# Six units of attention and three pieces of the layers per section instead of four and two, with the rows of 1/rms issued from ScalarE's queue

## The chip, the cores and the metric

The kernel runs on one core of one Trainium2 chip. A core has five engines that each work through a queue of their own: TensorE (PE, with PEld for its weight loads), VectorE (DVE), ScalarE (ACT), GpSimd (POOL) and SyncE (SP), which issues transfers. The metric is the device time of one execution in microseconds (us). The kernel before takes 531.6 us, the median of three runs (530.16 to 532.11). Its profile is of one execution with a span of 526.9 us. All arithmetic is in 32-bit floats.

## The reference, cut to what matters

Two blocks follow each other. Eight batches, twelve heads, 448 tokens, heads of 64.

```python
def rmsnorm(x, g):
    rms = np.sqrt(np.mean(x * x, axis=-1, keepdims=True) + 1e-06)
    return x / rms * g
q_n, k_n = rmsnorm(q, g_q), rmsnorm(k, g_k)
scores = scale * q_n @ k_n^T ; attn = softmax(scores)
x = attn @ v                     # as (batch, 448 tokens, 768)

scores = np.einsum('bsd,d->bs', x, w_gate)
for b in range(B):               # mixture of depths: 128 tokens of each batch
    top_idx = np.argpartition(-scores[b], 128)[:128]
    xe = x[b, top_idx]
    ye = np.maximum(xe @ w1, 0.0) @ w2        # 768 -> 1024 -> 768
    out[b, top_idx] = xe + sigmoid(scores[b, top_idx])[:, None] * ye
```

Tokens that are not chosen keep `x`. The two layers `w1` and `w2` are applied to the 128 chosen tokens alone.

## The kernel before, in words

**Tiling.** The work of attention is cut into 24 groups (eight batches of three), each with four heads, and each group into seven units of 64 keys. A unit `u` has a part `scores(u)`: four matmuls of 64x64 tiles into two PSUM buffers of the pool `ps_sc` (four in all), and two exponentials on ScalarE (L298) that write `p` (seven buffers). A part `values(u)` multiplies `p` with the values into `ps_av`, and `add_probs(u)` adds `p` into the group's sums on VectorE (L335) or, early, on GpSimd. A float matmul shows as two rows in the trace, so two units make 16 rows of scores and 16 of values.

**After a group.** `values_out` copies the result from PSUM on ScalarE, `sum_keys` sums the denominators on TensorE (den_ps, L367), `invert_sums` transposes them and takes the reciprocal (denT_ps, L392 and L394), and `to_tokens` transposes the result into tokens (x_ps, L410) and scales it into `x` on VectorE (L412). `last_tokens` does this for the second half of the group and then plans `gate` (L436, four VectorE products), and for a batch's last group `store_x` (L424) and `spread`.

**After a batch.** `ranks_of` transposes the gate scores to rows (row_ps, L465), which ScalarE copies (score_rows, L469); `count` finds each token's rank on VectorE (L479); `select` scatters the best 128 tokens to DRAM from GpSimd; `load_selected` reads them back as `xe`. `mixture` applies the layers to them, and is a generator: it is cut into ten pieces by its `yield`s. Two pieces transpose `xe` (L547, copied to `xeT` by ScalarE, L552), four multiply with `w1` (L575, relu on ScalarE after every second, L584), four with `w2` (L595, the result into `xe` by VectorE after every second, L604). All of them but the second write into the single PSUM buffer `moe_ps`. The tiles x_ps (its first half), den_ps and row_ps likewise share the single buffer of `ps_aux`.

**Norms.** The keys' 1/rms is a scale of the exponential. The queries' 1/rms has to be spread over the partitions: `squares` (ScalarE, L207), `sum_squares` (VectorE sum, L214, and a power on GpSimd, L217, 2.69 us each), then `rows_out` writes the 7 KB of 1/rms to DRAM (L228), `rows_in` reads them back as `bc`, every row to 64 partitions (L239), and `scale_q` multiplies the queries with them on VectorE (L248). A wait stands between: the read is issued only when the write has landed. The first two groups do without DRAM, by small matmuls (`scale_q_early`).

**The order.** Nothing is reordered: each engine takes its instructions as the Python code emits them. The main loop goes by sections. A section `q` first emits scores and values of its units, two by two, values lagging by two units, and then as many pieces of a mixture as the section has halves. With `HALVES = 2` a section has `PER = 4` units and two pieces, and 168 units make 42 sections. Around the pieces stand `opening(q, place)`, which takes the next of the tasks after a group, and `run(slots)`, which emits what was planned with `at(slot, ...)`: a slot is a unit, and the slots of a half are emitted around that half's piece. `prepare` plans squares, sums, `rows_out` and `rows_in` of group `n` from a slot about 20 units ahead of its first score, and `scale_q` 6 units ahead of it (in the first groups, 11 slots after the squares). `piece` starts a mixture when its batch is ready; while `q in begin`, in the first sections, no mixture that is past its second piece goes on in a section's second half. Loads of tokens, queries, keys, values and weights, the store of `x`, and the rows of 1/rms all go through SyncE's queue.

Of the kernel before, what the change touches and what calls it, by code (L numbers as in the profile page):

```python
# [68 lines left out]
def fast(  # L69
# [21 lines left out]
    nc = tc.nc  # L91

    B, NP, _, S = loads.src["qT"].shape
    CP = 112
    NJ = S // CP
    D = 64
# [59 lines left out]
    for c in range(2):  # L156
        nc.vector.memset(pick_pair[D * c : D * (c + 1), c : c + 1], 1.0)
    nc.vector.scalar_tensor_tensor(
        out=gg, in0=loads.gcol[:, 0:1], scalar=scale, in1=loads.gcol[:, 1:2], op0=OP.mult, op1=OP.mult
# [43 lines left out]
    def squares(n, i):  # L203
        t = get("tok", n, i)
        sq = sqs[(2 * n + i) % 2]
        for h in [slice(0, 1), slice(1, 2)] if (n, i) == (0, 0) else [slice(0, 2)]:
            nc.scalar.activation(out=sq[:, h, :, 0:D], in_=t[:, h], func=AF.Square, scale=scale)  # L207
        sss[n, i] = norm_pool.tile([128, 2, NI], F32, name="ss", bufs=4)
        return sq

    def sum_squares(n, i, sq):
        ss = sss.pop((n, i))
        for h in [slice(0, 1), slice(1, 2)] if (n, i) == (0, 0) else [slice(0, 2)]:
            nc.vector.tensor_reduce(out=ss[:, h], in_=sq[:, h], axis=AX.X, op=OP.add)  # L214
        rinv = norm_pool.tile([128, 2, NI], F32, name="rinv", bufs=8)
        flat = "p h i -> p (h i)"
        nc.gpsimd.tensor_tensor(  # L217
            out=rinv.rearrange(flat),
            in0=ss.rearrange(flat),
            in1=neg_half.to_broadcast([128, 2 * NI]),  # L220
            op=OP.pow,
        )
        rinvs[n, i] = rinv

    def rows_out(n):

        rows = dram_pool.tile([2, 2 * S], F32, name="rows", bufs=3)
        nc.sync.dma_start(  # L228
            out=rows.rearrange("h (p i) -> p h i", i=NI), in_=rinvs.pop((n, 0))
        )  # L230
        bcs[n] = rows

    def rows_in(n):

        rows = bcs[n]
        bc = norm_pool.tile([128, 2, S], F32, name="bc")
        for hh in range(2):
            src = rows[hh].rearrange("(c s) -> c s", c=2)
            nc.sync.dma_start(  # L239
                out=bc[D * hh : D * (hh + 1)],  # L240
                in_=dataclasses.replace(src, ap=[[0, D]] + [list(x) for x in src.ap]),
            )
        bcs[n] = bc

    def scale_q(n):
# [153 lines left out]
    def to_tokens(n, c):  # L399
        b = n // NG  # L400
        if b not in xs:
            xs[b] = x_pool.tile([CP, NJ, DX], F32, name="x")
        t = xTs.pop((n, c))
        shape = [128, NJ, 128]
        if c == 1 and not before_layers(now[0]):
            ps = ps_sc.tile(shape, F32, tag="sc", name="x_ps")
        else:
            ps = aux(shape, "x_ps")
        for j in range(NJ):
            nc.tensor.transpose(out=ps[:CP, j, :], in_=t[:, j, :], identity=ident)  # L410
        col = (n % NG * 2 + c) * 128
        nc.vector.tensor_tensor(  # L412
            out=xs[b][:, :, col : col + 128].rearrange("p j (h d) -> p j h d", d=D),
            in0=ps[:CP].rearrange("p j (h d) -> p j h d", d=D),
            in1=rdens[n][:, :, :, c, None].to_broadcast([CP, NJ, 2, D]),
            op=OP.mult,
        )
# [208 lines left out]

    HALVES = 2
    PER = 2 * HALVES  # L630
    units = n_groups * NI
    todo, tasks = {}, []

    def at(slot, fn, *args):
        todo.setdefault(slot, []).append(lambda: fn(*args))
# [6 lines left out]
    def opening(q, place):  # L642
        now[:] = q, place
        for _ in range(2):
            for i, (when, fn) in enumerate(tasks[:2]):
                if when <= (q, place):
                    tasks.pop(i)
                    waited = len(dens)
                    fn()
                    if place == 0 and len(dens) < waited:  # L650

                        break
                    return
                if i == 0 and dens:

                    return

    def prepare(n, slot):
        sq = {}
        for i in range(2):  # L660
            at(slot + 2 * i, lambda i=i: sq.setdefault(i, squares(n, i)))
            at(slot + 2 * i + 1, lambda i=i: sum_squares(n, i, sq.pop(i)))

        at(slot + (7 if n > 2 else 6), rows_out, n)
        at(slot + (10 if n > 5 else 9 if n > 2 else 8), rows_in, n)

    for n in range(1, n_groups):
        s0 = NI * n
        if n > 2:
            at(max(s0 - 26, 4 * (n - 3)), load, "tok", n, 0)  # L670
            at(max(s0 - 26, 4 * (n - 3)), load, "tok", n, 1)
        if n > 1:
            at(max(s0 - 13, 2), load, "qT", n)
            at(max(s0 - 11, 2), load, "kT", n)
            at(max(s0 - 11, 2), load, "v", n)
            first = max(s0 - (20 if n > 5 else 17), 0)
            prepare(n, first)
            at(max(s0 - 6, first + 11), scale_q, n)
# [5 lines left out]
    def finish(n, q):  # L684

        if n == n_groups - 1:
            for fn, args in ((sum_keys, (n,)), (invert_sums, (n,)), (to_tokens, (n, 0))):
                task((q, 1), fn, *args)
            task((q, 1), last_tokens, n)
            return  # L690
        task((q, 1), sum_keys, n)
        task((q + 1, 0), to_tokens, n, 0)
        task((q + 1, 1), last_tokens, n)
# [10 lines left out]
    def soon():  # L704

        q, place = now
        return PER * q + 2 * place if PER * q < units else -9

    def last_tokens(n):
        to_tokens(n, 1)  # L710
        b, g = divmod(n, NG)
        s = soon()
        at(s, gate, n)
        if g < NG - 1:
            return
        at(s, store_x, b)
        at(s + 1, spread, b)
        q, place = now

        when = (q + 1 + place // 2, 0) if b < B - 1 else (q + 1, 1)  # L720
        tasks.insert(0, (when, lambda: ranks_of(b)))

    def ranks_of(b):
        score_rows(b)
        s = soon()
        at(s, count, b, (0, 1))
        at(s + 1, count, b, (2, 3))
        at(s + 2, annotate, b)
        at(s + 2, select, b)
        at(s + 8 if s >= 0 else s + 3, load_selected, b)  # L730
        ready[b] = max((s + 8) // PER + 1, first_ff(b) - 1 if b else 0) if b < B - 1 else 0

    def first_ff(b):


        return -(-(units + 2 * PER - NG * NI * (B - 2 - b)) // PER)
# [34 lines left out]
    def piece(q):  # L771

        nonlocal moe, done
        if q in begin and pieces[0] > 2 and half == 1:
            return False
        pieces[0] += 1
        if next(moe, moe) is not moe:
            return True
        if ready.get(done, q + 1) > q:
            return False  # L780
        moe = mixture(done)
        done += 1
        pieces[0] = 1
        next(moe)
        return True


    begin = range(first_ff(0) + 1)
    pieces = [0]
    waiting = list(range(units))  # L790
    moe, ready, done, q = iter(()), {}, 0, 0
    while done < B or tasks:
        now[:] = q, 0
        k = PER * q
        for half in range(HALVES):
            for u in (k + 2 * half, k + 2 * half + 1):
                if u < units:
                    scores(u)
            run_values(k + 2 * half - 1, q)
        opening(q, 0)  # L800
        for half in range(HALVES):
            slots = (k + 2 * half, k + 2 * half + 1)
            if not short(q):
                run(slots)
            some = piece(q)
            spare[0] = not some and half == 0
            if some or half == 0 or len(tasks) > 2:
                opening(q, half + 1)
            spare[0] = False
            run(slots)  # L810
        q += 1
# [533 lines left out]
```

## Time and profile before

| what | value |
|---|---|
| time, median of 3 | 531.6 us |
| span of the profile | 526.9 us |
| TensorE busy | 507.6 us, 96% |
| VectorE, ScalarE, GpSimd busy | 63%, 53%, 36% |
| attention on TensorE (L289, L313) | 154.8 and 147.1 us busy |
| layers on TensorE (`w1` L575 while attention runs, `w2` L595) | 69.3 and 61.3 us busy |
| share of the 16 DMA engines, 11 to 97 us | 0.84 |
| the same, 97 to 467 us | 0.55 |
| write of the rows, issue to landing | 5.4 us, median of 22 |
| read of the rows, issue to landing | 6.4 us, median of 44 |

The lengths of TensorE's rows overlap, because matmuls are pipelined; what a run of them costs is read from its start to the start of the next. In a row of the timeline stand its start, its length, the engine, the line, the operation, the tile it writes and those it reads, the shape, how many instructions are merged, and in brackets the idle time of the engine before it and what ended that. SPq rows are SyncE's issuing of transfers, not the transfers. The first 97 us have attention and loads alone, from 104 us on layers and attention alternate, and after 467 us the layers of the last two batches are left.

### The profile page before, as it was taken

The numbers are of one execution on the slowest core, as the hardware profiler recorded it, in microseconds if no ns is written. First come the engines' busy times: TensorE is split into PE (matmuls) and PEld (weight loads), VectorE is DVE, ScalarE is ACT, GpSimd is POOL, SyncE is SP. The second block draws the span as 40 slices with busy tenths as digits, with TensorE's granted clock in tenths as the row PEclk, the third lists the DMA queues.
The fourth block names the chain that finished last, engine by engine and source line by source line (L and its number), as shares of the span: only waits on it lengthen the run. The fifth ranks groups of instructions, "written<-read, shape, count | busy, mean of one in ns | idle before, by whom it ended". The sixth has DMA issues, their size and how long they took to land.

```text
span 526.9 us, 11121 instructions
## 1 busy us (share of the span) xinstructions
PE 507.6 (96%) x4482; PEld 298.8 (57%) x4482; DVE 334.2 (63%) x638; ACT 278.1 (53%) x507; POOL 191.8 (36%) x109
## 2 busy tenths in 40 slices
PE   6999997999999999999999999998999999999995
PEld 5544343565744476546654467644664448659694
DVE  4566879579846896658666787467947487336101
ACT  4886873857644845456644585645463474401100
POOL 4956866623512454132712424304621003002102
PEclk9999998999999999999999999999999999999998
DMA  8968779799764297526846396537542231104100
GB/s 304 382 217 291 244 224 345 251 291 340 200 187 161 82 291 232 163 94 192 260 136 183 87 297 211 159 103 223 195 131 71 70 136 31 31 1 143 53 32 35
DMA packets 43405, 93.21 MB, mean 177 GB/s; under 512 B 11059, under 2 KB 23348, under 8 KB 43346
## 3 DMA queue, kind: packets, MB, share of 16 engines
q1 hardware_dynamic: 39938, 86.11, 52.1%
q0 software_dynamic: 3264, 6.31, 3.5%
q8 instruction: 37, 0.61, 0.5%
q14 instruction: 22, 0.18, 0.1%
q10 hardware_dynamic: 144, 0.00, 0.0%
HBM read 74.93 MB, written 25.35 MB: 190 GB/s over the span
## 4 chain that ended last, share of the span: by engine, by line
PE 89%; DVE 4%; DMA 2%; ACT 2%; issue 2%; POOL 0%; DVEq 0%; SPq 0%; ACTq 0%; POOLq 0%
PE sc L289 24%; PE av L313 22%; PE moe_ps L575 13%; PE moe_ps L595 11%; PE sc L595 4%; PE x_ps L410 4%; PE sc L575 4%; PE den_ps L367 3%; DMA bc<-rows 2%; PE denT_ps L392 1%; ACT p L298 1%; DVE sum L335 1%; PE warm_ps L164 1%; DVE ss L214 1%; DVE x L412 1%
## 5 line engine op out<-in xcount | busy, mean ns | idle before, releaser
L298 ACT ACTIVATE p<-sc,rinv 128x448 f32<-128x448 f32 x336 | 186.6, 642 | 106.3 <-PE sc L289 92.5
L217 POOL TENSOR_TENSOR rinv<-ss,neg_half 128x14 f32<-128x14 f32 x48 | 128.8, 2689 | 198.3 <-DVE ss L214 170.6
L289 PE MATMUL sc<-qT,kT 64*64 64x448 f32 x1344 | 154.8, 549 | 1.1 <-DVE qT L268 0.4
L313 PE MATMUL av<-p,v 64*64 64x448 f32 x1344 | 147.1, 537 | 0.0
L335 DVE TENSOR_TENSOR sum<-sum,p 128x896 f32<-128x896 f32 x101 | 111.6, 1105 | 7.2 <-ACT p L298 0.9
L313 PEld LDWEIGHTS av<-p,v 64*64 64x64 f32 x1344 | 60.1, 133 | 67.6 <-issue 56.9
L289 PEld LDWEIGHTS sc<-qT,kT 64*64 64x64 f32 x1344 | 54.3, 133 | 70.9 <-issue 47.0
L214 DVE TENSOR_REDUCE ss<-sq 128x14 f32<-128x910 f32 (+1 forms) x49 | 52.4, 1074 | 33.9 <-ACT sq L207 33.9
L575 PE MATMUL moe_ps<-xeT,w 128*128 128x128 f32 x576 | 69.3, 277 | 0.0
L575 PEld LDWEIGHTS moe_ps<-xeT,w 128*128 128x128 f32 x576 | 66.2, 192 | 5.3 <-issue 5.3
L595 PE MATMUL moe_ps<-w,hT 128*128 128x384 f32 x176 | 61.3, 491 | 0.4 <-DVE xe L604 0.3
L412 DVE TENSOR_TENSOR x<-x_ps,rden 112x512 f32<-112x512 f32 x48 | 32.8, 690 | 37.2 <-PE x_ps L410 36.4
L506 POOL DMA_INDIRECT selected<-x,rank x32 | 33.6, 1050 | 47.3 <-DVE x L498 39.3
L207 ACT ACTIVATE sq<-tok 128x896 f32<-128x896 f32 (+1 forms) x49 | 46.4, 951 | 5.7 <-DMA tok<-in_tok_dram 3.7
L595 PEld LDWEIGHTS moe_ps<-w,hT 128*128 128x128 f32 x176 | 31.7, 190 | 22.5 <-issue 2.5
L436 DVE SCALAR_TENSOR_TENSOR prod<-x,wg 112x256 f32<-112x256 f32 x96 | 41.5, 432 | 3.0
L614 POOL DMA_INDIRECT out_dram<-xe,row x10 | 11.6, 1164 | 81.1 <-DVE rden L394 47.3
L410 PE MATMUL x_ps<-ident,xT 128*112 128x128 f32 x192 | 29.5, 279 | 3.3 <-DVE rden L394 3.3
L335 DVE TENSOR_TENSOR sum<-p 128x896 f32<-128x896 f32 x24 | 25.9, 1078 | 5.2 <-ACT p L298 5.2
L604 DVE SCALAR_TENSOR_TENSOR xe<-sc,xe 128x384 f32<-128x384 f32 (+1 forms) x6 | 3.3, 550 | 40.6 <-PE sc L595 40.6
L410 PEld LDWEIGHTS x_ps<-ident,xT 128*112 128x112 f32 x192 | 21.8, 135 | 12.6 <-issue 7.7
L248 DVE SCALAR_TENSOR_TENSOR qT<-qT,gg,bc 128x896 f32<-128x896 f32 x22 | 25.2, 1147 | 5.1 <-DMA bc<-rows 5.1
(71 smaller groups left out, 311.0 us busy)
## 6 DMA issues: line engine op xcount, KB each, us to landing
tok<-in_tok_dram SPq DMA_DIRECT2D x48, 448.0 KB, 6.3
qT<-in_qT_dram SPq DMA_DIRECT2D x24, 448.0 KB, 6.2
kT<-in_kT_dram SPq DMA_DIRECT2D x24, 448.0 KB, 7.0
v<-in_vp_dram SPq DMA_DIRECT2D x24, 448.0 KB, 7.7
out_dram<-x SPq DMA_DIRECT2D x8, 1344.0 KB, 7.8
bc<-rows SPq DMA_DIRECT2D x44, 224.0 KB, 6.4
xe<-selected SPq DMA_DIRECT2D x8, 385.0 KB, 3.1
w<-in_moe_w_dram SPq DMA_DIRECT2D x6, 512.0 KB, 6.4
```

Of the source, the lines that this page charges most:

```text
L207: nc.scalar.activation(out=sq[:, h, :, 0:D], in_=t[:, h], func=AF.Square, scale=scale)
L214: nc.vector.tensor_reduce(out=ss[:, h], in_=sq[:, h], axis=AX.X, op=OP.add)
L217: nc.gpsimd.tensor_tensor(out=rinv.rearrange(flat), in0=ss.rearrange(flat), in1=neg_half.to_broadcast([128, 2 * NI]), op=OP.pow,)
L289: nc.tensor.matmul(out=scs[hh][D * c : D * (c + 1), 0:S], lhsT=get("kT", n)[r, c, D * i : D * (i + 1)], rhs=get("qT", n)[r, c, :], start=True,
L298: nc.scalar.activation(out=p[:, hh], in_=scs[hh][:, 0:S], func=AF.Exp, scale=rinvs[n, 1][:, hh, i : i + 1],)
L313: nc.tensor.matmul(out=avs[n][c][D * hh : D * (hh + 1), 0:S], lhsT=get("v", n)[r, hh, i, :], rhs=probs[u][r, hh], start=(i == 0), stop=(i ...
L335: nc.vector.tensor_tensor(out=sums[n], in0=probs.pop(u - 1) if begins else sums[n], in1=probs.pop(u), op=OP.add)
L410: nc.tensor.transpose(out=ps[:CP, j, :], in_=t[:, j, :], identity=ident)
L412: nc.vector.tensor_tensor(out=xs[b][:, :, col : col + 128].rearrange("p j (h d) -> p j h d", d=D), in0=ps[:CP].rearrange("p j (h d) -> p j ...
L436: nc.vector.scalar_tensor_tensor(out=prod, in0=xs[b][:, j, cols], scalar=1.0, in1=wg[:, cols], op0=OP.mult, op1=OP.mult, accum_out=gates[b ...
L575: nc.tensor.matmul(out=ps[:, 128 * i : 128 * i + n], lhsT=w1[:, dc, 128 * (f0 + i) : 128 * (f0 + i + 1)], rhs=xeT[:, dc, :n], start=(dc == 0),
L595: nc.tensor.matmul(out=ps[:n, :width], lhsT=hT[:, fc, :n], rhs=w2[:, fc, cols], start=(fc == 0), stop=(fc == NFC - 1),)
```

## The change

`HALVES` goes from 2 to 3, so that a section has six units and three pieces: fewer times from one kind of work to the other, more of each at a time. Three expressions that depend on the number of halves follow it (the place at which a batch's ranking is put, and the rule for the first sections). The rows of 1/rms are written and read back from ScalarE's queue instead of SyncE's, and read with one transfer of 448 KB for both halves of the partitions instead of two of 224 KB. Their slots are 6 and 8 after the first squares for every group, where they were up to 7 and 10. This takes them out of the queue in which they waited among the loads.

```diff
     def rows_out(n):
         rows = dram_pool.tile([2, 2 * S], F32, name="rows", bufs=3)
-        nc.sync.dma_start(
+        nc.scalar.dma_start(
             out=rows.rearrange("h (p i) -> p h i", i=NI), in_=rinvs.pop((n, 0))
         )
...
         bc = norm_pool.tile([128, 2, S], F32, name="bc")
-        for hh in range(2):
-            src = rows[hh].rearrange("(c s) -> c s", c=2)
-            nc.sync.dma_start(
-                out=bc[D * hh : D * (hh + 1)],
-                in_=dataclasses.replace(src, ap=[[0, D]] + [list(x) for x in src.ap]),
-            )
+        (h_step, _), row = [list(x) for x in rows.ap]
+        nc.scalar.dma_start(
+            out=bc.rearrange("d c s -> d (c s)"),
+            in_=dataclasses.replace(rows[:, :], ap=[[h_step, 2], [0, D], row]),
+        )
         bcs[n] = bc
...
-    HALVES = 2
+    HALVES = 3
     PER = 2 * HALVES
...
-        at(slot + (7 if n > 2 else 6), rows_out, n)
-        at(slot + (10 if n > 5 else 9 if n > 2 else 8), rows_in, n)
+        at(slot + 6, rows_out, n)
+        at(slot + 8, rows_in, n)
...
-        when = (q + 1 + place // 2, 0) if b < B - 1 else (q + 1, 1)
+        when = (q + 1, place // HALVES) if b < B - 1 else (q + 1, 1)
...
-        if q in begin and pieces[0] > 2 and half == 1:
+        if q in begin and pieces[0] > 2 and half > 0:
             return False
```

## The prediction

> **What bounds the kernel now.** I read the page's busy shares first, then its chain of waits, then TensorE's timeline from end to end, then the queue of SyncE.
>
> ```profile
> PE 507.6 (96%) x4482; PEld 298.8 (57%) x4482; DVE 334.2 (63%) x638; ACT 278.1 (53%) x507; POOL 191.8 (36%) x109
> ...
> PE 89%; DVE 4%; DMA 2%; ACT 2%; issue 2%; POOL 0%; DVEq 0%; SPq 0%; ACTq 0%; POOLq 0%
> ```
>
> TensorE is the bound: busy 96% of the span and 89% of the chain. The change leaves its matmuls as they are, so all that can move is the time between them. TensorE's timeline shows one whole section in the steady part (start, length):
>
> ```profile
> 334.34 1.74 PE L289 MATMUL sc<-qT,kT 64*64 64x448 f32 x16
> 335.89 1.68 PE L313 MATMUL av<-p,v 64*64 64x448 f32 x16
> 337.40 1.68 PE L289 MATMUL sc<-qT,kT 64*64 64x448 f32 x16
> 338.90 1.68 PE L313 MATMUL av<-p,v 64*64 64x448 f32 x16
> 340.51 0.65 PE L410 MATMUL x_ps<-ident,xT 128*112 128x128 f32 x4
> 341.00 2.75 PE L595 MATMUL moe_ps<-w,hT 128*128 128x384 f32 x8
> 343.58 0.60 PE L410 MATMUL x_ps<-ident,xT 128*112 128x128 f32 x4
> 344.02 2.75 PE L595 MATMUL moe_ps<-w,hT 128*128 128x384 f32 x8
> 346.69 0.59 PE L367 MATMUL den_ps<-sum,pick_pair 128*32 128x224 f32 x8
> 347.21 1.73 PE L289 MATMUL sc<-qT,kT 64*64 64x448 f32 x16
> ```
>
> Read starts, not lengths: a run of 16 scores or values takes 1.50 us from start to start, four transposes 0.44, a piece of the second layer 2.58, one of the first 2.68. These parts sum to 12.4 us, the section is 12.87 long. I did this for every section: length from start to start, less the parts at their least spacing. The best sections keep 0.30 us over, and that is the price of going from the 64x64 tiles of attention to the 128-row work and back. The 32 sections from 97.07 to 466.61 keep 18.6 us in all: 32 x 0.30 = 9.6, about 4.2 where the 128x32 sums stand between pieces (0.4 more than 0.30 in each such section), and 4.8 real waits. The ten from 11.39 to 97.07 keep 14.3: 3.0 of switching, about 1 of those sums, 10 of waits.
>
> Two of the steady waits, from the same timeline:
>
> ```profile
> 156.14 2.75 PE L595 MATMUL moe_ps<-w,hT 128*128 128x384 f32 x8
> 158.72 0.60 PE L410 MATMUL x_ps<-ident,xT 128*112 128x128 f32 x4
> 159.60 2.85 PE L595 MATMUL moe_ps<-w,hT 128*128 128x384 f32 x8 [0.28 <-DVE xe L604]
> ...
> 365.64 0.49 PE L547 MATMUL moe_ps<-ident,xe 128*128 128x128 f32 x3
> 367.45 0.59 PE L367 MATMUL den_ps<-sum,pick_pair 128*32 128x224 f32 x8 [1.32 <-ACT score_rows L469]
> ```
>
> The layers own one PSUM buffer (moe_ps). When a piece ends its use of it and the next piece starts in the same section, TensorE waits for VectorE or ScalarE to read it out: 159.60 - 158.72 = 0.88 for work of 0.44. That is rare here, since two pieces per section and buffers used for two pieces mostly put the handover at a section's end, beneath the next attention.
>
> The queue of SyncE, and what the rows of 1/rms did to VectorE and TensorE in the timeline of all engines:
>
> ```profile
> 22.83 0.38 SPq L228 DMA_DIRECT2D rows<-rinv  x1
> ...
> 27.83 1.17 SPq L239 DMA_DIRECT2D bc<-rows  x2
> ```
>
> ```profile
> 79.45 1.15 DVE L248 SCALAR_TENSOR_TENSOR qT<-qT,gg,bc 128x896 f32<-128x896 f32 x1 [2.35 <-DMA bc<-rows]
> ...
> 87.26 1.10 PE L410 MATMUL x_ps<-ident,xT 128*112 128x128 f32 x4 [3.27 <-DVE rden L394]
> ```
>
> Five us pass from write to read. The late rows at 79.45 hold VectorE, and then TensorE at 87.26: the sections from 76.49 and 88.29 lose 5.7 us to waits.
>
> **What the Trainium skill says.** TensorEngine Tiling (Array Packing), Key Properties: changing the tiling mode drains TensorE. The trace agrees, 0.30 us a section. DMA: Bandwidth & Descriptors, Issuing engines are not separate DMA queues: a DMA from another engine runs on the same 16 engines and saves only the sequencer's time. So ScalarE's queue buys no bandwidth; it frees SyncE's, whose L239 waited 32.0 us for rows. Same page, Two DMAs through the same engine are not ordered: the issuer must wait for the first DMA's semaphore before it issues the dependent one. The 5.0 us above show it on SyncE; after the change it is ScalarE that stands there. TensorE: Matmul & The Clock Gate, What's actually happening: an idle window of about 3.4 us drops the clock. After the 3.27 us wait above, the next 16 scores took 2.85 us instead of 1.73.
>
> **The change, part by part.**
>
> *Fewer switches.* 42 sections become 28; in TensorE's order 13 returns from attention fall away. 13 x 0.30 = 3.9 us gained, all on the path.
>
> *Three pieces per section.* A mixture is ten pieces, and its buffer changes hands after pieces 2, 4, 6, 8 and 10. With threes these points fall inside sections. In the order of the changed program, numbering sections from 0, I find per batch pair of seven sections (12 to 18, 19 to 25, and 26 and 27 begin a third), with ScalarE and VectorE walked through by their rows (relu 0.60, xeT copy 0.48, xe 0.62, square 0.95, cmp 0.77, gate 4 x 0.47, sums 1.1):
> - 12, 19, 26: row_ps, a transpose pair, x_ps, then the first piece of w1. x_ps waits for score_rows, and the piece for xeT copies that stand behind a row load and a square on ScalarE. From attention's end: row_ps is done at 0.8, the pair at 1.1, score_rows at 1.6, so x_ps waits 0.5; ScalarE goes on with the exponential of parts 0.2, the load 0.45, the square 0.95, and copies xeT until 3.6 and 4.1, where TensorE comes at 2.9: 0.8 more. Bounds 0.4 (0.36 was lost so at 307.21) and 1.5; I take 1.2, thrice, 3.6.
> - 14, 21: xe is behind a gate (1.9) and a sum of squares (1.1) on VectorE, which can start on them only after the second x at 4.4: xe ends at 8.0, and TensorE comes at 6.8. 0.3 to 1.25, I take 1.0, twice, 2.0.
> - 15, 22: xe with one x_ps between: 0.44 measured above, plus ScalarE's late xeT; 0.7, twice, 1.4.
> - 13, 20, 27 and 16, 23 and 10, 17, 24: relu with 0.44 to 0.52 of other work between; 0.3 each, eight times, 2.4.
>
> That is 9.4 against 4.8 of waits before: 4.6 lost. All these lie on TensorE's path, since inside a section nothing else is queued.
>
> *The rows on ScalarE.* Issuing costs nothing: 2 x 0.45 us per group lie beside pieces of 2.6 us, and ScalarE idles there. The waits are new. SyncE ran ahead of the others and issued as soon as 1/rms was there. ScalarE reaches the issue only after the section's exponentials, and what is queued behind it are den copies, relus and the next section's exponentials, for which TensorE's score buffers wait. From group 6 on, the load comes six slots before its use, a whole section, so nothing is late. In 2/3 of the groups write and load fall in one section, and ScalarE waits there for the landing (1.8 us is the one small DMA of ScalarE's queue, 5.4 the median of rows on SyncE's). Pieces of 2.6 us hide it: 0 to 1 each, I take 0 in sum beyond the 1.2 and 0.7 above.
>
> Groups 2 to 7 are another matter: no pieces run yet, and scaling of the queries follows the load within the same section.
> - Group 2: from the end of attention in section 1, write 0.4, landing 1.8 to 5.4, load landing 3.3 to 6.4 (least and median), scaling 1.15: 6.7 to 13.3 us. TensorE wants the queries after 1.4 of sums and 3.0 of attention. Loss 2.3 to 8.9; I take 4.0.
> - Group 3: on VectorE a sum 1.45, x and squares 3.8, gate 1.9 and scaling 1.15 make 8.3 us, TensorE comes at 6.4: 2.
> - Group 5: 0 to 1.6; I take 1.
> - Group 7: the write waits for a 1/rms of its own section (sum 1.1 and pow 2.69 after VectorE's backlog, some 5.1 us), ScalarE stands, and TensorE's second scores come at 4.3, the buffers at 6.6: 2.3, more if its load of tokens is late.
>
> 9.3 us against about 7.3 that go (the 10 of waits less 2.7 of the start, which stay; 5.7 of them are those above). Add 1 for an idle clock: 3.0 lost.
>
> *One load of 448 KB instead of two of 224.* The same bytes; the second issue (0.5 us) was on SyncE. Nothing. *The ranking's place, the start rule:* these move one row_ps by a place. Nothing.
>
> *The tail.* Two more pieces of the second layer come after attention, and leave the sections: equal. The xeT pair now stands next to its piece: 0.4 lost. The wait of the last batch stays hidden, as the same 18 us of pieces lie between row_ps and its transposes.
>
> Sum: -3.9 + 4.6 + 3.0 + 0.4 = +4.1, 535.7 us.
>
> **Rivals.** *Faster:* VectorE and ScalarE keep up, steady waits stay at 4.8, and the rows, off a crowded queue, end the 5.7 at 76 to 92 with new early losses of about 5. -3.9 - 0.7 = 527 us. For it: the engines are at 63% and 53%, and SyncE's loads come earlier. Against it: the handovers are fixed by the order of the queues. *No change:* handovers of 0.3 alone (+1) and early losses at their low ends, 531.6. *Much slower:* rows land in 5.4 and TensorE loses 0.5 to 1 for each of the 15 groups with write and load in one section, beside the early losses: 535.7 + 8 = 544. For it: ScalarE's tokens and rows share 16 engines at 0.8 to 0.9 load until 150 us.
>
> **How the numbers follow.** Forecast 45%, much slower 10%, no change 18%, faster 27%. The range 526 to 543 leaves out most of the last of the slow case and gains over 1%. Slower by over 0.5% is 55%, same 18%, faster 27%.
>
> **What would show it.** TensorE's best sections of six still keep 0.30 over; x_ps or L595 with idle time after xe and relu in mid-section; sc<-qT,kT waiting for qT at 35 to 45 us; ScalarE idle with a DMA of rows named. I am wrong if handovers show no wait, or if bc lands within about 4 us of attention's end in section 1.

## The result and the profile after

The changed kernel takes 620.2 us (median of four runs, 619.18 to 623.64), beside 530.9 us of the kernel before on the same chip: a ratio of 1.169, with a 95% interval of 1.164 to 1.175. The prediction was 535.7 us in a range of 526 to 543. It named the right side and missed the size by 84.5 us.

The page of the changed kernel: the busy shares, and the chain of waits by engine.

```profile
PE 529.3 (86%) x4482; PEld 315.4 (51%) x4482; DVE 331.9 (54%) x638; ACT 278.6 (45%) x507; POOL 194.5 (32%) x109
...
PE 64%; DMA 13%; issue 10%; POOL 5%; ACT 4%; DVE 3%; ACTq 1%; DVEq 0%; POOLq 0%
```

TensorE still has 4482 matmuls, but it holds 64% of the chain instead of 89%. DMA went from 2% to 13%, and "issue", time in which the profile shows no releaser, from 2% to 10%. The page's groups name who was idle, after the last bar (idle time before the group, then what ended most of it):

```profile
L288 PE MATMUL sc<-qT,kT 64*64 64x448 f32 x1344 | 167.5, 572 | 62.1 <-issue 44.8
...
L207 ACT ACTIVATE sq<-tok 128x896 f32<-128x896 f32 (+1 forms) x49 | 46.2, 950 | 58.8 <-DMA rows<-rinv 19.7
...
L247 DVE SCALAR_TENSOR_TENSOR qT<-qT,gg,bc 128x896 f32<-128x896 f32 x22 | 25.2, 1147 | 70.8 <-DMA bc<-rows 70.8
```

Two of these groups before:

```profile
L289 PE MATMUL sc<-qT,kT 64*64 64x448 f32 x1344 | 154.8, 549 | 1.1 <-DVE qT L268 0.4
...
L248 DVE SCALAR_TENSOR_TENSOR qT<-qT,gg,bc 128x896 f32<-128x896 f32 x22 | 25.2, 1147 | 5.1 <-DMA bc<-rows 5.1
```

L247 is the scaling of the queries (L248 before). VectorE stood 70.8 us ahead of it for `bc`, where it was 5.1 before. The matmuls of the scores come next: 62.1 us of idle time ahead of them, 1.1 before. And ScalarE, ahead of its squares, stood 19.7 us for the write of the rows. The first of these waits, in the timeline of all engines:

```profile
34.38 1.73 PE L288 MATMUL sc<-qT,kT 64*64 64x448 f32 x16
...
34.58 1.10 ACTq L238 DMA_DIRECT2D bc<-rows  x1
...
35.94 1.68 PE L312 MATMUL av<-p,v 64*64 64x448 f32 x16
...
52.83 1.15 DVE L247 SCALAR_TENSOR_TENSOR qT<-qT,gg,bc 128x896 f32<-128x896 f32 x1 [18.03 <-DMA bc<-rows]
...
54.09 3.04 PE L288 MATMUL sc<-qT,kT 64*64 64x448 f32 x16 [16.46 <-issue]
```

The load is issued at 34.58 and its data are used at 52.83, 18.2 us later; before, a load of rows took 3.3 to 10.5 us with a median of 6.4. TensorE stops for 16.46 us and then runs its next sixteen at 3.04 us instead of 1.73, at a granted clock of 0.54 from 54 to 57 us. What the DMA engines do in the middle of this wait, by window (columns: busy us and count of PE, PEld, DVE, ACT, POOL, then clock, DMA share, GB/s):

```profile
40.00:52.00 12.00, 0.00 (x0) 0.00 (x0) 0.00 (x0) 0.00 (x0) 0.00 (x0) 0.50 0.27 96
```

The same stretch of the kernel before:

```profile
40.00:52.00 12.00, 11.78 (x132) 5.47 (x124) 8.44 (x18) 8.67 (x16) 8.17 (x4) 1.00 0.94 313
```

No engine computes, and the DMA engines are not crowded either: a share of 0.27. So the load is slow while most of the sixteen engines are idle. Counted in the packets of the trace, a load of 448 KB is 128 packets of 3584 bytes, 0.14 us each in the median, spread over 9.2 to 17.7 us; averaged over a load, never more than 2.04 are in flight. Two engines carry it. It also shares these two: from 43 to 51 us the trace has 2.0 packets in flight, and 30% of that time goes to packets of SyncE's loads that are still unfinished. This fits that most loads take longer than the 9.2 us of the shortest.

What this does to the next transfer of the queue shows later, in the steady part:

```profile
397.99 0.51 ACTq L238 DMA_DIRECT2D bc<-rows  x1
...
401.91 0.36 ACTq L228 DMA_DIRECT2D rows<-rinv  x1
...
417.47 0.51 ACTq L238 DMA_DIRECT2D bc<-rows  x1
418.03 0.60 ACT L583 ACTIVATE hT<-moe_ps 128x512 f32<-128x512 f32 x1 [4.64 <-DMA rows<-rinv]
...
418.68 1.65 PE L574 MATMUL moe_ps<-xeT,w 128*128 128x128 f32 x6 [2.78 <-ACT hT L583]
```

The 7 KB of group n+1 are written from 401.91, while the load of group n is still running until 416.3. Of the write's 274 packets 238 are through by 406; the last 36 start between 414.7 and 416.8. These 36 are about an eighth of the write, the part that two of sixteen engines would carry: as I read it, the shares that fall to the two loaded engines have to wait. ScalarE stands until 417.47 before it can issue the next load, its relu (L583) is 4.64 us late, and TensorE 2.78 us.

### The profile page after: what moved, and what is told of

It reads as the page before. It is cut to its first block, busy times and chain, and to the rows that moved or that the text cites. A ratio compares the mean times of both kernels' runs of the same rounds, so it can differ in the third digit from the quotient of the medians.

```text
span 617.3 us, 11131 instructions
## 1 busy us (share of the span) xinstructions
PE 529.3 (86%) x4482; PEld 315.4 (51%) x4482; DVE 331.9 (54%) x638; ACT 278.6 (45%) x507; POOL 194.5 (32%) x109
## 4 chain that ended last, share of the span: by engine, by line
PE 64%; DMA 13%; issue 10%; POOL 5%; ACT 4%; DVE 3%; ACTq 1%; DVEq 0%; POOLq 0%
PE sc L288 18%; PE av L312 16%; PE moe_ps L574 8%; DMA rows<-rinv 8%; PE moe_ps L594 7%; PE sc L594 4%; POOL rinv L217 4%; PE sc L574 4%; DMA v<-in_vp_dram 2%; PE x_ps L409 2%; ACT p L297 1%; PE den_ps L366 1%; DMA tok<-in_tok_dram 1%; PE denT_ps L391 1%; DVE ss L214 1%
## 5 line engine op out<-in xcount | busy, mean ns | idle before, releaser
L288 PE MATMUL sc<-qT,kT 64*64 64x448 f32 x1344 | 167.5, 572 | 62.1 <-issue 44.8
L312 PE MATMUL av<-p,v 64*64 64x448 f32 x1344 | 156.1, 555 | 0.0
L288 PEld LDWEIGHTS sc<-qT,kT 64*64 64x64 f32 x1344 | 59.9, 137 | 138.3 <-issue 86.1
L312 PEld LDWEIGHTS av<-p,v 64*64 64x64 f32 x1344 | 66.3, 139 | 69.5 <-issue 55.9
L574 PE MATMUL moe_ps<-xeT,w 128*128 128x128 f32 x576 | 74.2, 289 | 8.7 <-ACT hT L583 8.3
L574 PEld LDWEIGHTS moe_ps<-xeT,w 128*128 128x128 f32 x576 | 71.0, 203 | 13.4 <-ACT hT L583 9.9
L207 ACT ACTIVATE sq<-tok 128x896 f32<-128x896 f32 (+1 forms) x49 | 46.2, 950 | 58.8 <-DMA rows<-rinv 19.7
L247 DVE SCALAR_TENSOR_TENSOR qT<-qT,gg,bc 128x896 f32<-128x896 f32 x22 | 25.2, 1147 | 70.8 <-DMA bc<-rows 70.8
L594 PE MATMUL moe_ps<-w,hT 128*128 128x384 f32 x160 | 55.7, 491 | 2.7 <-DVE xe L603 1.9
L411 DVE TENSOR_TENSOR x<-x_ps,rden 112x512 f32<-112x512 f32 x48 | 33.0, 689 | 41.7 <-PE x_ps L409 37.3
L594 PEld LDWEIGHTS moe_ps<-w,hT 128*128 128x128 f32 x160 | 28.8, 190 | 21.2 <-DVE xe L603 2.8
L393 DVE RECIPROCAL rden<-denT_ps 112x16 f32<-112x16 f32 x24 | 6.1, 256 | 51.3 <-PE denT_ps L391 51.3
L594 PE MATMUL sc<-w,hT 128*128 128x384 f32 (+1 forms) x112 | 32.1, 441 | 0.0
```

The source lines that it names most:

```text
L288: nc.tensor.matmul(out=scs[hh][D * c : D * (c + 1), 0:S], lhsT=get("kT", n)[r, c, D * i : D * (i + 1)], rhs=get("qT", n)[r, c, :], start=True,
L312: nc.tensor.matmul(out=avs[n][c][D * hh : D * (hh + 1), 0:S], lhsT=get("v", n)[r, hh, i, :], rhs=probs[u][r, hh], start=(i == 0), stop=(i ...
L574: nc.tensor.matmul(out=ps[:, 128 * i : 128 * i + n], lhsT=w1[:, dc, 128 * (f0 + i) : 128 * (f0 + i + 1)], rhs=xeT[:, dc, :n], start=(dc == 0),
L594: nc.tensor.matmul(out=ps[:n, :width], lhsT=hT[:, fc, :n], rhs=w2[:, fc, cols], start=(fc == 0), stop=(fc == NFC - 1),)
```

## The experiments

My first theory of the result (A): the merged load is slow by itself, since its pattern in DRAM begins with an extent of 2. The Trainium skill, DMA: Bandwidth & Descriptors, Why a DMA increments its semaphore by 16 and not by 1, says how many engines carry a DMA: the largest number up to 16 that divides the slowest extent of both sides. The load's sides begin with 128 and with 2, so two engines; the two old loads began with 64 and 64, so sixteen. The packets above agree. The rivals: the queue of ScalarE is the cause, or the long sections are. All times stand against the kernel before on the same chip, 529.8 to 530.7 us.

**Undo the merged load in the changed kernel.**

```diff
-        in_=dataclasses.replace(rows[:, :], ap=[[h_step, 2], [0, D], row]),
+        for hh in range(2):      # two loads of 224 KB, still from ScalarE
...
+            in_=dataclasses.replace(src, ap=[[0, D]] + [list(x) for x in src.ap]),
```

> The changed kernel, with the one load of 448 KB back as two of 224 KB, still from ScalarE's queue. Theory A (the load's first dimension of 2 leaves it on two DMA engines, which is what takes 18 us): the load lands in 3 to 7 us, ScalarE no longer stands, and the time is that of the prediction's own account, 527 to 543 us. Rival B (ScalarE's queue itself: its transfers are slow, or its waits for the landing stop the exponentials): still 590 us or more. Rival C (sections of six leave no time between load and scaling): still 590 us or more, with VectorE waiting for bc.

Measured: 556.1 us, ratio 1.047 (1.043 to 1.052). 64 us go with this one edit. The packets of both loads together now lie within 2.1 to 5.6 us, with up to 11.4 in flight. But 556 lies above the 527 to 543 of theory A, and 25 us above the kernel before: something else costs these 25.

**Do the merged load alone in the kernel before.** The same edit the other way, on SyncE.

> The kernel before with one thing changed: one load of 448 KB from SyncE's queue instead of two. Sections of four, slots as before. Theory A: the load takes 9 us at least (64 rows of 0.14 us on each of two engines), VectorE waits for bc in most groups, and loads behind it are late: 560 to 620 us. Rivals B and C: 529 to 533 us, since neither ScalarE's queue nor the sections are touched.

Measured: 574.8 us, ratio 1.083 (1.081 to 1.086): 44 us from merging two loads into one, nothing else changed. VectorE's wait for `bc` is 72.7 us here, 70.8 in the changed kernel.

**The pattern without the merging.** The kernel before, two loads of 224 KB from SyncE, with the repeated row written in two levels:

```diff
-                in_=dataclasses.replace(src, ap=[[0, D]] + [list(x) for x in src.ap]),
+                in_=dataclasses.replace(src, ap=[[0, 2], [0, D // 2]] + [list(x) for x in src.ap]),
```

> The kernel before with two loads of 224 KB from SyncE as before, but each written with a first dimension of 2 on the side it reads (2 x 32 rows instead of 64). Bytes, number of transfers, queue and order are the same. Theory A: both loads on the same two engines, so as slow as the one load: 560 to 620 us, within 2% of the kernel before with one load. If instead the number of transfers or their size matters: 529 to 533 us.

Measured: 582.0 us, ratio 1.098 (1.094 to 1.101). Number, size and queue of the transfers are as before, every byte goes to the same place, and 51 us are lost, within 2% of the merged load's time as theory A asked. With 4 and 16 in the place of 2:

> The kernel before, with the source of each of its two loads written as 4 x 16 x row instead of 64 x row: the same bytes to the same partitions, from SyncE. two_shares had 2 x 32 x row and 582.0 us. Theory A: the first extent of the pattern sets how many DMA engines take part: four engines need half the time of two, about 64 packets x 0.14 us / 4 = 2.2 us at least for a load and 4.5 us for both, where two needed 9, so most of the 51 us go: 531 to 548 us, the rows landing some 7 to 9 us after their issue. Rival B: it is the broken pattern as such (a repeated row split in two levels) that is slow, whatever its first extent: 570 to 590 us.

> The kernel before, with the source of each of its two loads written as 16 x 4 x row. The first extent was 2 in two_shares (582.0 us) and 4 in four_shares (553.4 us). Theory A: only the first extent counts, and with 16 the load runs on all sixteen engines as it did with 64: 528 to 533 us. Rival B: every pattern in which the repeated row is split in two levels is slower: 537 us or above.

Measured: 553.4 us (ratio 1.043, 1.038 to 1.049) with 4 and 529.0 us (0.998, 0.997 to 0.999) with 16. A first extent of 2, 4 and 16 costs +51, +24 and nothing. Rival B, that a broken pattern is slow whatever its extent, falls with the 16. The value for 4 lies above what I expected, since even half the time is late for the first groups; four_shares in the timeline:

```profile
40.13 1.15 DVE L248 SCALAR_TENSOR_TENSOR qT<-qT,gg,bc 128x896 f32<-128x896 f32 x1 [10.17 <-DMA bc<-rows]
41.39 1.74 PE L289 MATMUL sc<-qT,kT 64*64 64x448 f32 x16 [2.88 <-issue]
```

2.88 us of TensorE's time at the place where the changed kernel lost 16.46, and two_shares 7.14. The packets say the same: wherever those of the rows are alone in flight, there are 2.0 to 2.1 at once in two_shares and one_load_sync and 4.0 to 4.1 in four_shares. The cause of the 64 us is settled: the number of DMA engines.

**Sections of six alone.** `HALVES = 3` and the expressions that follow it (two, and not three as I had counted) in the kernel before; rows on SyncE, two loads, old slots.

> The kernel before with sections of six units and three pieces (and the two rules that follow), rows of 1/rms from SyncE with two loads, in their old slots. By the prediction's account of sections and handovers alone: 3.9 us gained, 4.6 lost, 0.4 in the tail, and early losses of up to 6 as the scaling comes in the section of the load: 530 to 538 us. Rival C: 590 us or more. If three pieces are cheap to hand over: 524 to 529 us.

Measured: 550.4 us, ratio 1.037 (1.031 to 1.043). This missed: 20 us where I had accounted for about 1. The largest piece is one section from 72.26, which keeps 12.3 us over its parts. In the timeline of all engines:

```profile
77.10 0.69 SPq L424 DMA_DIRECT2D out_dram<-x  x1
78.31 2.42 SPq L239 DMA_DIRECT2D bc<-rows  x2
...
87.10 1.15 DVE L248 SCALAR_TENSOR_TENSOR qT<-qT,gg,bc 128x896 f32<-128x896 f32 x1 [5.51 <-DMA bc<-rows]
88.36 1.77 PE L289 MATMUL sc<-qT,kT 64*64 64x448 f32 x8 [6.62 <-issue]
```

With longer sections a load at the old slots falls into the section in which its queries are scaled: nine us before its use, behind the store of a whole batch. New theory: rows that come late for their scaling are most of this loss, and the slots decide it. Two ways to bring them earlier, both on SyncE with two loads: everything of a group three slots earlier (rows_earlier), and the changed kernel with its slots 6 and 8 put back on SyncE (sync_sections).

```diff
-            first = max(s0 - (20 if n > 5 else 17), 0)
+            first = max(s0 - (23 if n > 5 else 20), 0)      # rows_earlier
```

> sections_only (sections of six, rows on SyncE, two loads, old slots) with the squares, the write and the load of each group planned three slots earlier, half a section. Theory A: about half of the 22 us that sections of six lost were rows that came late for the scaling of queries (two sections of 12.3 and 6.5 us over, and others before unit 48): 536 to 545 us. Rival B: the loss is in the handovers of the layers' buffer and of the score buffers, and the rows are only seen beside them: 547 to 553 us. Rival C: the tokens of which the squares are taken are late then (their load is planned at the same slot as before), so nothing is won: 548 us or above, with ScalarE's squares waiting for tokens.

> The changed kernel with the write of the rows and two loads of 224 KB put back on SyncE: sections of six and slots 6 and 8 stay. It differs from sections_only (550.4 us) in the slots alone, and from two_loads (556.1 us) in the queue alone. Theory A: the queue is what two_loads lost, and an earlier load helps the sections in which the scaling of the queries waited for it (2.5 us of waiting at 159.43 of sections_only): 544 to 550 us. Rival B: the slots are what two_loads lost (the write is issued before its 1/rms is ready and holds the queue): 553 to 559 us.

Measured: 537.8 us (ratio 1.015, 1.010 to 1.020) and 536.5 us (1.012, 1.006 to 1.017). Either takes back 13 to 14 us, so the theory holds, and more than I had expected of the slots. sync_sections has no wait of VectorE for `bc` left. Together:

> sync_sections (536.5 us) with the squares, the write and the load of each group planned three slots earlier, as in rows_earlier (537.8 us), which has the old slots. Theory A: both cure the same thing, the load in the section of the scaling, and what is left of sections of six is the handovers and the early part: 534 to 538 us. Rival B: the cures add: 527 to 533 us, level with the kernel before.

Measured: 538.3 us, ratio 1.016 (1.014 to 1.019): they cure the same thing. All three kernels stay 7 to 9 us above the kernel before.

**The slots alone**, in the kernel before with its sections of four:

```diff
-        at(slot + (7 if n > 2 else 6), rows_out, n)
-        at(slot + (10 if n > 5 else 9 if n > 2 else 8), rows_in, n)
+        at(slot + 6, rows_out, n)
+        at(slot + 8, rows_in, n)
```

> The kernel before with slots 6 and 8 for every group, nothing else: sections of four, SyncE, two loads. With sections of six these slots were worth 14 us (sync_sections 536.5 against sections_only 550.4). Theory A: that was because the load had fallen into the section in which the queries are scaled; with four slots to a section the old slot lies a whole section ahead, so nothing is won here: 527 to 533 us. Rival B: the slots are good as such: under 526 us. Rival C: the write is planned before its 1/rms is ready and holds SyncE's queue: 534 to 540 us.

Measured: 525.2 us, ratio 0.991 (0.989 to 0.994). Faster than both kernels; this run's theory A expected nothing and falls. The gain sits in one place, the late rows that the prediction had shown at 79.45 and 87.26. slots_only in the timeline:

```profile
76.43 1.74 PE L289 MATMUL sc<-qT,kT 64*64 64x448 f32 x16
76.97 1.15 DVE L248 SCALAR_TENSOR_TENSOR qT<-qT,gg,bc 128x896 f32<-128x896 f32 x1
...
84.76 0.65 PE L410 MATMUL x_ps<-ident,xT 128*112 128x128 f32 x4 [1.29 <-DVE rden L394]
...
85.34 1.73 PE L289 MATMUL sc<-qT,kT 64*64 64x448 f32 x16
...
93.21 1.74 PE L289 MATMUL sc<-qT,kT 64*64 64x448 f32 x16
```

The scaling no longer waits, the transposes wait 1.29 us instead of 3.27, and the two sections from there take 8.91 and 7.87 us instead of 11.80 and 8.78: 3.8 us, all of the difference of the two spans (526.9 and 523.1).

**ScalarE's queue alone**, in the kernel before with its old slots, and the write alone on ScalarE in sections of six:

```diff
     def rows_out(n):
-        nc.sync.dma_start(
+        nc.scalar.dma_start(
     def rows_in(n):
-            nc.sync.dma_start(
+            nc.scalar.dma_start(      # left on SyncE in write_on_scalar
```

> The kernel before, with nothing changed but the queue: the write of the rows and the two loads of 224 KB are issued from ScalarE; sections of four units, old slots. two_loads stands 5.8 us above sections_only (556.1 against 550.4). Theory A: these 5.8 us are ScalarE standing at the issue of a row transfer, so the queue alone costs about as much in sections of four: 533 to 540 us. Rival B: standing on ScalarE costs only in long sections or with the earlier slots, so 529 to 533 us here. Rival C: the queue alone is worse, since the loads of SyncE come earlier and collide: above 541 us.

> two_loads with the two loads back on SyncE; the write stays on ScalarE, so ScalarE no longer stands until the write has landed, only until its 1/rms is there. two_loads had 556.1 us, sync_sections, which has the write on SyncE too, 536.5 us. Theory A: nearly all of the 19.6 us is ScalarE standing for the landing and what queues behind it: 535 to 541 us. Rival B: it is the write's own wait for 1/rms on ScalarE: 548 to 557 us. Rival C: it is that SyncE's loads run ahead of the rows once these are out of its queue: between, 541 to 548 us.

Measured: 540.6 us (ratio 1.019, 1.014 to 1.024) and 538.1 us (1.017, 1.014 to 1.019). The queue costs 10.8 us with sections of four, just above the 3 to 10 that I expected, and 19.6 us with sections of six (two_loads less sync_sections). With the write alone on ScalarE it costs 1.7 us, which lies within the intervals: so it is the loads there that cost, 18 us. Putting them back on SyncE does two things at once, though: ScalarE no longer stands for the write's landing in front of a load, and SyncE stands there instead and runs ahead less. No run parts the two. scalar_queue shows one stand of ScalarE:

```profile
94.83 0.84 SPq L61 DMA_DIRECT2D tok<-in_tok_dram  x2
...
97.45 0.37 ACTq L228 DMA_DIRECT2D rows<-rinv  x1
...
105.32 1.16 ACTq L239 DMA_DIRECT2D bc<-rows  x2
106.86 2.21 ACT L298 ACTIVATE p<-sc,rinv 128x448 f32<-128x448 f32 x4 [6.96 <-issue]
107.55 3.78 PE L289 MATMUL sc<-qT,kT 64*64 64x448 f32 x16 [7.45 <-ACT p L298]
```

SyncE, free of the rows, has just issued a run of loads (94.39 to 97.18); the 7 KB behind them need 7.9 us. ScalarE stands in front of the load at 105.32, the exponentials behind it are 6.96 us late, the score buffers fill, TensorE loses 7.45 us, and its clock is 0.50 from 107.5 to 111. The write's last packet ends at 104.32, so this stand is for the landing. two_loads shows two stands in a row:

```profile
158.91 0.37 ACTq L228 DMA_DIRECT2D rows<-rinv  x1
159.37 0.95 ACT L207 ACTIVATE sq<-tok 128x896 f32<-128x896 f32 x1 [4.81 <-DMA v<-in_vp_dram]
...
164.99 1.10 ACTq L239 DMA_DIRECT2D bc<-rows  x2
...
166.19 0.95 ACT L207 ACTIVATE sq<-tok 128x896 f32<-128x896 f32 x1 [5.87 <-DMA kT<-in_kT_dram]
...
167.97 3.52 PE L289 MATMUL sc<-qT,kT 64*64 64x448 f32 x16 [4.53 <-ACT p L298]
```

The first, 4.81 us, stands in front of the write. The trace names the landing of v, a load of SyncE's queue which the rows do not read; their 1/rms was ready at 153.15. The program counts its transfers on a few semaphores that both queues share: the trace has this load of v (issued at 149.21) and the write on the same one, on which v was complete at 158.83, just before the write went. The second ends at 164.99. For the 5.87 us the line names kT, but the write's last packet ends at 164.40 and its semaphore moves last at 164.90: this stand is for the landing of the rows.

Sorted in this way, by packets and semaphores, ScalarE's stands at the transfers of the rows in two_loads come to about 25 us: 11 until the write had landed, in four of 22 groups; 10 until a load of SyncE's queue that used the same semaphore was in; 4 for 1/rms in front of the write. That is ScalarE's time. How much of TensorE's 18 us belongs to each kind was not told apart by a run.

## Why the prediction was wrong

The four parts of the change, each as the difference of two measured kernels in a row:

| part | kernels | predicted | measured |
|---|---|---|---|
| slots 6 and 8 | before, slots_only | with the queue | -4.6 |
| sections of six | slots_only, sync_sections | -3.9 + 4.6 + 0.4 = +1.1 | +11.3 |
| rows from ScalarE's queue | sync_sections, two_loads | +3.0, with the slots | +19.6 |
| one load for two | two_loads, changed kernel | 0 | +64.1 |
| sum | | +4.1 | +90.4 |

The rows join kernels from different chips, on which the kernel before took 529.8 to 530.9 us; measured directly, the change costs 89.3. Each part also depends on what stands beside it. Alone in the kernel before, the merged load cost 44.1 us, the sections 19.7, the queue 10.8 and the slots -4.6, 70.0 in sum: about 19 more come from their meeting.

**The step that failed** is "One load of 448 KB instead of two of 224. The same bytes; the second issue (0.5 us) was on SyncE. Nothing." It holds 64 of the 86 us between the two sums. I took a transfer's time from its bytes and the crowding of the engines, and read no cost out of the shape of its pattern. The diff showed it: `[[h_step, 2], [0, D], row]` where `[[0, D]]` had stood. The page of the skill that I cited for the queues states the rule in another section, and its price follows from the packets: 128 x 0.14 us / 2 = 9.0 us at least, and 9.2 to 17.7 were measured; with sixteen engines 1.1, and 2.1 to 5.6 were measured. All that the prediction says of landings (3.3 to 6.4 us, "six slots before its use, a whole section, so nothing is late") rested on the old loads' times; with two loads, in two_loads, VectorE waits for `bc` once, for group 2. The stops cost more than their length, too. I had put 1 us for an idle clock: TensorE is busy 21.7 us longer with the same 4482 matmuls (529.3 against 507.6), at a mean clock of 0.939.

**Rows on ScalarE.** Where I looked for losses they came. Group 2 was to lose 4.0 us (2.3 to 8.9); two_loads stops 6.56 us at that place, with `bc` landing by its packets at 41.7. Group 7 was to lose 2.3, since ScalarE would stand at its write for a late 1/rms; two_loads loses 3.37 us at 102.80, but there luck has a part: the write of group 7 went at 101.70 without a stand, and ScalarE had stood at the load of group 6 until 99.20, for a load of tokens on the same semaphore. These two stops of two_loads in the timeline:

```profile
43.87 3.27 PE L289 MATMUL sc<-qT,kT 64*64 64x448 f32 x16 [6.56 <-issue]
...
102.80 3.34 PE L289 MATMUL sc<-qT,kT 64*64 64x448 f32 x16 [3.37 <-ACT p L298]
```

What failed is "0 in sum" for the 15 groups with write and load in one section. I bounded a landing by 5.4 us, a median, and took pieces of 2.6 us as cover; it was 7.9 us in the example above, behind loads that SyncE, as I read it, issued because it had been freed (no run tested that). In two_loads the writes' last packets ended 1.1 to 8.6 us after their issue, and four of them left ScalarE standing for 11 us. For a transfer that waits on a semaphore shared with SyncE's loads, another 10 us of standing, I had no term at all. The much slower rival had the first mechanism at 8 us. And the gain set against it was real but belonged to the slots: slots_only has it without the queue.

**Three pieces per section.** The handovers came where I put them, mostly smaller. sync_sections in the timeline:

```profile
197.90 0.65 PE L410 MATMUL x_ps<-ident,xT 128*112 128x128 f32 x4 [0.30 <-ACT score_rows L469]
...
215.36 2.95 PE L575 MATMUL moe_ps<-xeT,w 128*128 128x128 f32 x24 [0.17 <-ACT hT L584]
...
238.05 2.85 PE L595 MATMUL moe_ps<-w,hT 128*128 128x384 f32 x8 [0.97 <-DVE xe L604]
...
254.69 0.55 PE L547 MATMUL moe_ps<-ident,xe 128*128 128x128 f32 x3 [0.28 <-DVE xe L604]
```

I had 1.2 for the first with its xeT copies, 0.3, 1.0 and 0.7. To size the whole, I took each kernel's time from its first section of attention to unit 48, and from there to the end of the span:

| kernel | to unit 48 | from unit 48 |
|---|---|---|
| before | 105.1 | 410.4 |
| slots_only | 101.1 | 410.4 |
| sync_sections | 108.9 | 414.7 |
| two_loads | 118.5 | 423.8 |
| changed | 158.0 | 447.8 |

From unit 48 on, where nearly all handovers and ten of the thirteen saved switches lie, sections of six cost 4.2 us; my terms for that part come to about 2. The other 7.8 us are early, and there I had no term for the sections as such, only for the rows. The trace of sync_sections shows one stop of that kind:

```profile
100.76 2.08 POOL L329 TENSOR_TENSOR tok<-p 128x896 f32<-128x896 f32 x1
...
102.87 1.16 ACT L298 ACTIVATE p<-sc,rinv 128x448 f32<-128x448 f32 x2 [6.33 <-POOL tok L329]
...
103.56 2.29 PE L289 MATMUL sc<-qT,kT 64*64 64x448 f32 x8 [2.55 <-ACT p L298]
```

GpSimd adds some `p` in the early part. This add stands behind the four scatters of `select` (95.44 to 100.74), so the buffer of `p` stays taken, and exponential and scores wait. That reading is from the trace alone; no run took the adds off GpSimd. Nor was the 0.30 for a switch tested by itself.

**Direction and rivals.** Slower by over 0.5% was right, and would have been with two loads too (556.1 us), but 64 of the 90 us come from a term that I had put at nothing. No rival came near 620, for none touched the load's shape. The stop I had named as a sign, scores waiting for qT at 35 to 45 us, is there, as is ScalarE idle with a transfer of rows named.

## What to carry to other kernels

Read a transfer's pattern before its bytes: merging two loads can put a 2 in front and leave two of sixteen DMA engines to do the work, so look at packets in flight, or at a low DMA share while somebody waits for a landing. Be wary of putting a transfer that depends on another transfer on an engine that computes: here its exponentials stood behind the landing, and behind loads of another queue that shared a semaphore, and the loads there cost 18 us. When sections are made longer, work planned in slots falls into other sections than before: here the planning was worth 14 us with six units and 4.6 with four, and the best kernel of the study (525.2 us) changes the slots and nothing else.

## What the runs showed of the hardware that was not expected

- The number of DMA engines follows the first extent of the pattern even where a repeated row is read again and again: first extents 2, 4, 16 and 64 gave 582.0, 553.4, 529.0 and 529.8 us for the same bytes.
- A slow load on two engines delays a later transfer of its queue that runs on all: 7 KB took 15.6 us from issue to the point at which the next load could go, with 36 of 274 packets late, against a median of 5.4 us from issue to landing before.
- One engine's issue can wait for another queue's load that neither side reads, because both use one semaphore: in two_loads the write of the rows waited 4.3 us at 158.91 for a load of v.
- A stop of TensorE costs more than its length, and by more than the prediction had put: after 16.46 us of waiting the next sixteen scores took 3.04 us instead of 1.73. The mean clock granted to the changed kernel was 0.939, 0.994 before.
